# Attention and two feed-forward blocks on one core: weight work assigned to other steps, and the second token block's operands made at other times and on another engine

## The chip, the cores and the metric

One Trainium2 chip, one of its cores. The time of a kernel is the device time of one launch in microseconds (us); several runs are made and their median is given. The engines named below are TensorE (PE, the matrix engine), VectorE (DVE), ScalarE (ACT), GpSimd (POOL) and SyncE (SP), whose queue issues nearly all DMAs.

## The reference

Three parts follow each other on 2304 tokens (4 sequences of 576) of 512 features:

```python
# attention, 8 heads of 64
cum    = np.cumsum(np.maximum(s, 0), axis=-1)
scores = q @ k.T / sqrt(64) + np.minimum(-(cum[..., None] - cum[..., None, :]), 0)
x      = softmax(causal(scores)) @ v          # 2304 x 512
# first block, 512 -> 2048 -> 512
h = x @ w_in;  x = np.maximum(0.01 * h, h) @ w_out
# second block, 512 -> 2048 -> 512, with weights of its own
h = x @ w_in2; y = (np.maximum(h, 0) + np.log1p(np.exp(-np.abs(h)))) @ w_out2
```

The weights come as 64-bit floats, which the kernel turns into 32-bit floats with integer operations.

## The kernel before, in words

Every product is made from a high and a low part of each operand (hi x hi, hi x lo, lo x hi, three products on PE). High parts are made by a copy on ACT, low parts by a subtraction on DVE or POOL.

**Attention** takes the first quarter of the span (to about 244 us) and is not touched.

**The first block** (the "first half" of what follows) runs over 68 steps, written out in `steps`. The 16 blocks of 128 hidden units are taken in four groups of four (`G = 4`): group 0 has 8 steps for the tokens that attention left over (2 chunks of 384, steps 0 to 7), groups 1 to 3 have 20 steps each (5 chunks of 512, 512, 256, 512 and 512 tokens, four hidden blocks each), beginning at steps 8, 28 and 48 (`begin`). A step n (loop at L898) does, in this order: the products into a hidden bank (`h_mm`, L145); the work that was put off to this step (`tick`); the leaky activation on ACT (L826); the entries of `plan` for this step; and the output products of step n - 3 (`out_mm`, L846). After the fourth hidden block of a chunk, `out_mm` adds four banks to `acc` on DVE (L853; a copy on ACT in group 0). Output products rotate through five banks of which a chunk needs four, so the next chunk's first output step needs the banks that these additions free.

All engines take their instructions in the order in which this program issues them. What stands in `plan` (L856 to L896) is:
- `own` (L864): the conversions (`split_w`) of this block's weights for the next group, eight per group, "i" for the input weights and "o" for the output weights. DVE does three or four instructions (L114 to L123), ACT three, POOL one or two.
- `spare` (L872 to L877): the 32 conversions (`prepare`) of the second block's weights, in the order of `blocks`: (j, e, "i" or "o") for j = 0 to 7. `prepare` is put on step n: two ACT instructions (L728, L729) then, the four DVE instructions of `convert` (L732 to L735) in step n + 1, the high part on ACT (L708) in n + 1 and the low part on POOL (L712) in n + 2, with two stores to `w2d` in DRAM by SP. The second "i" block of a pair also brings four half-width sums on DVE at step n + 2 (L751 to L757), which make two more operands. The raw load of a block is issued two steps ahead, into one of four buffers.
- the operands of the second block's first token block (L883 to L896), from step 59 on: sums on DVE (L794), high parts on ACT (L797), low parts on DVE or POOL (L801).

Before, `spare` spread 22 of the 32 blocks evenly over the free steps of groups 1 and 2, and 10 over the first 13 steps of group 3.

**The second block** (the "second half") does its input products as seven instead of eight products of half-size blocks: four token chunks in two token blocks (`sb` 0 and 1, `PAIRS`), operands B11, B12, B21, B22 and the sums T1 = B12 - B11, T2 = B22 - T1, T3 = B22 - B12, T4 = B21 - T2. Seven operands (B12 is only used in sums) are split into high and low parts, which lie in eight places of `xh` and `xl` (`slots`, `home`); the sums overwrite their sources in `acc`. `Quad(sb, j)` does the seven products (L1013) for two hidden blocks and joins them on DVE (L1030); four `Unit`s then make the activation: four ACT instructions, then DVE (L958, L961), POOL `correct` (L964), ACT high part (L970), POOL low part (L974). `outputs` multiplies by the output weights (L1068) and DVE adds to `acc` (L1076). A `Plain` does the same for the 256 tokens that are in neither block, with ordinary products (L1095). `emit_out` and the plain products share three banks.

The order is a list of events with a time `t` (`on`), sorted at the end; one unit of `t` is meant as one product of a quad. Quad n's products take 7 units; then come the outputs of quad n - 1 (8 units), the plain products (2.1) and the outputs of the plain before (2). The second token block's operands are made around quad 7 (`t7`, L1140 to L1148): four sums and four low parts, for each of two halves (`kp`), on DVE; the other three low parts on POOL. `fetch` loads the prepared weights back from `w2d`, on SP: "i" 6 units ahead of a quad, "o" 1 unit after its start.

Of the kernel before, what the change touches and what calls it, by code (L numbers as in the profile page):

```python
# [13 lines left out]
F32R = mybir.dt.float32r  # L14
AF = mybir.ActivationFunctionType
ALU = mybir.AluOpType
PSUM = bass.MemoryType.PSUM

P = 128
# [12 lines left out]
def attn_moe_moe(ctx, tc, q, k, v, s, w1i, w1o, w2i, w2o, out):  # L32
    nc = tc.nc
# [7 lines left out]
    NG = NF // G  # L41
# [9 lines left out]
    def pool(name, bufs=1, **kw):  # L51
        return tc.tile_pool(name=name, bufs=bufs, **kw)
# [616 lines left out]
    enter = lambda stage, nm, **kw: stages[stage].enter_context(pool(nm, **kw))  # L669
# [26 lines left out]
    begin = {}  # L696
# [4 lines left out]
    NJ = NF // 2  # L701
# [61 lines left out]
    def split_x(c):  # L763
# [7 lines left out]
    slots = [(r, c) for c in (*PAIRS[0], *PAIRS[1]) for r in (0, 2)]  # L771
    home = [
        {"B11": 0, "T2": 1, "T3": 2, "T1": 3, "B21": 4, "T4": 5, "B22": 6},
        {"B11": 7, "T2": 0, "T3": 1, "T1": 2, "B21": 3, "T4": 4, "B22": 5},
    ]
    PRODUCTS = [
        ("A11", "B11"), ("S2", "T2"), ("S3", "T3"), ("S1", "T1"), ("A12", "B21"), ("A22", "T4"), ("S4", "B22")
    ]

    def operand(sb, nm, kp):  # L780
        r, c = slots[home[sb][nm]]
        c = slice(c, c + 512)
        return xh[:, r + kp, c], xl[:, r + kp, c]

    def source(sb, nm, kp):
        i, k = {"B11": (0, 0), "T1": (0, 0), "T2": (0, 0), "B12": (1, 0), "T3": (1, 0), "B21": (0, 2), "T4": (0, 2), "B22": (1, 2)}[nm]
        c = PAIRS[sb][i]
        return acc[:, k + kp, c:c + 512]

    def combine(sb, nm, kp, queue=nc.vector):  # L790

        a, b = {"T1": ("B12", "B11"), "T3": ("B22", "B12"), "T2": ("B22", "T1"), "T4": ("B21", "T2")}[nm]
        a, b = source(sb, a, kp), source(sb, b, kp)
        queue.tensor_tensor(source(sb, nm, kp), a, b, op=ALU.subtract)  # L794

    def x_high(sb, nm, kp):
        nc.scalar.activation(operand(sb, nm, kp)[0], source(sb, nm, kp), AF.Copy)  # L797

    def x_low(sb, nm, kp, queue=nc.vector):
        hi, lo = operand(sb, nm, kp)  # L800
        queue.tensor_tensor(lo, source(sb, nm, kp), hi.bitcast(F32), op=ALU.subtract)  # L801
# [56 lines left out]
    def at(n, fn, *args):  # L858
        plan.setdefault(n, []).append((fn, args))

    taken = set()
    for g in range(1, NG):
        a = begin[g - 1]
        own = (2, 5, 8, 11, 15, 18, 16, 19) if g > 1 else (None,) * 4 + (3, 6, 4, 7)  # L864
        for j, n in enumerate(own):
            if n is not None:
                w = (0, g * G + j // 2, "io"[j % 2])
                at(max(a + n - 2, 0), load_w, *w)
                at(a + n, split_w, *w, (1, 1, 1, 1, 2, 2))
                taken.add(a + n)  # L870
    blocks = [(j, e, nm) for j in range(NJ) for e, nm in ((0, "i"), (1, "i"), (0, "o"), (1, "o"))]
    a, z = begin[1], begin[NG - 1]  # L872
    spare = [[n for n in r if n not in taken] for r in (range(a, z), range(z, z + 13))]
    spare = [r[k * len(r) // m] for r, m in zip(spare, (22, 10)) for k in range(m)]
    for n, x in zip(spare, blocks):
        at(max(n - 2, 0), load_w, 1, 2 * x[0] + x[1], x[2])
        at(n, prepare, n, *x)  # L877
# [5 lines left out]
    k = begin[NG - 1, chunks[1]] + G + LAG  # L883
    z = len(steps) - 1
    follow = {"B11": "T1", "T1": "T3", "T3": "T2"}
    for nm, n in (("B11", k), ("T1", k + 2), ("T3", k + 4), ("B21", k + 5), ("T2", k + 6), ("T4", z - 1), ("B22", z)):
        for kp in range(2):
            m = min(n + kp, z)
            if nm == "T4":
                at(m, combine, 0, nm, kp)  # L890
            at(m, x_high, 0, nm, kp)
            at(m, x_low, 0, nm, kp, nc.gpsimd if nm in ("T3", "B21") else nc.vector)
            if nm in follow:
                at(m, combine, 0, follow[nm], kp)
# [19 lines left out]

    wpools.append(enter(1, "wpool1", bufs=2))
    lpool = enter(1, "lpool", bufs=3, side="right")
    gpools = [enter(1, "gpool1", bufs=3, side="right"), gpool]
    order = [0]
    events = []
# [2 lines left out]
    def on(t, fn, *args):  # L922
        events.append((t, len(events), fn, args))
# [63 lines left out]
    class Quad:  # L987
# [13 lines left out]
        def product(self, n, name):  # L1001
            a, b = PRODUCTS[n]
            if name not in self.ps:
                tag, bufs = next(banks["ps_h"]) if self.first_one else TAGS[name]
                self.ps[name] = psA.tile([P, 512], F32, tag=tag, name="ps_h", bufs=bufs)
            k, half = {"A11": (0, 0), "A12": (0, 1), "A21": (1, 0), "A22": (1, 1),
                       "S1": (2, 0), "S2": (2, 1), "S3": (3, 0), "S4": (3, 1)}[a]
            wh, wl = ready[self.sb, self.j, "i"][k]
            for kp in range(2):
                w = slice(half * HALF + kp * P, half * HALF + (kp + 1) * P)  # L1010
                hi, lo = operand(self.sb, b, kp)
                for m, (x, y) in enumerate(((wh[:, w], hi), (wh[:, w], lo), (wl[:, w], hi))):
                    nc.tensor.matmul(  # L1013
                        self.ps[name], x, y, start=n < 4 and kp == 0 and m == 0, stop=kp == 1 and m == 2,
                        skip_group_check=n >= 4,
                    )
# [96 lines left out]
    quads = [Quad(sb, j) for sb in range(2) for j in range(NJ)]  # L1113
    plains = [Plain(j) for j in range(NJ)]
    t = 0
    for n, q in enumerate(quads):
        q.at(t)
        if n + 1 < len(quads):
            j = quads[n + 1].sb, quads[n + 1].j
            on(t - 6 if n else -1, fetch, *j, "i")  # L1120
            on(t + 1, fetch, *j, "o")
        if n == NJ - 1:
            t7 = t
        t += 7
        if n == 0:
            for i in range(LAG, 0, -1):
                on(t, out_mm, len(steps) - i)
                t += 2
        else:
            quads[n - 1].outputs(t)  # L1130
            t += 8
        if n < NJ:
            plains[n].at(t)
            t += 2.1
        if 0 < n <= NJ:
            plains[n - 1].outputs(t)
            t += 2
    quads[-1].outputs(t)

    for kp in range(2):  # L1140
        b = t7 + 1.25 * kp
        for n, nm in ((-8, "B11"), (3.2, "T1"), (5.7, "T3"), (8.2, "T2"), (10.7, "B21"), (13.2, "T4"), (15.7, "B22")):
            if nm in ("T2", "T4"):
                on(b + n - 0.9, combine, 1, nm, kp)
            on(b + n, x_high, 1, nm, kp)
            on(b + n + 0.8, x_low, 1, nm, kp, nc.gpsimd if nm in ("T3", "B21", "B22") else nc.vector)
        on(b - 5, combine, 1, "T1", kp)
        on(b - 2, combine, 1, "T3", kp)  # L1148

    for t, _, fn, args in sorted(events, key=lambda x: x[:2]):  # L1150
        fn(*args)
# [48 lines left out]
```

## Time and profile before

| | us |
|---|---|
| median of 3 runs (lowest, highest) | 962.31 (961.06, 964.36) |
| the profiled execution | 961.56 |
| its span, first to last instruction | 959.8 |
| PE busy, of the span | 945.1 |
| DVE busy | 672.5 |
| ACT busy | 574.7 |
| POOL busy | 553.2 |

The profile is of one execution. Busy times of PE include the overlap of pipelined products, so a pause is seen best from the start of one product to the start of the next. "x12" in a row is a count; what stands behind "<-" in brackets is the idle time in front of an instruction and what ended it. L numbers are lines of the kernel.

### The profile page before, as it was taken

To read this page: it belongs to the slowest core of one execution; us is meant where nothing else is said; L and a number is where in the kernel's file an instruction comes from. 1 tells how busy PE (TensorE), PEld (TensorE's weight loads), DVE (VectorE), ACT (ScalarE), POOL (GpSimd) and SP (SyncE) were. 2 spreads that over 40 slices of the span, in tenths; PEclk is the share of its full clock that TensorE was granted. 3 is DMA by queue.
4 is the path that set the end of the run, shared out by engine and by line. 5 is a ranking of instruction groups with operands and counts; after the bars stand their busy time and mean duration, and the time that the engine had idled before them with its cause. 6 is when DMAs were issued, how large, how long until landed. Compare 5 with 4: busy or idle time off the path is not lost.

```text
span 959.8 us, 15357 instructions
## 1 busy us (share of the span) xinstructions
PE 945.1 (98%) x5173; PEld 767.8 (80%) x5173; DVE 672.5 (70%) x1306; ACT 574.7 (60%) x1185; POOL 553.2 (58%) x536
## 2 busy tenths in 40 slices
PE   9999999999999999998999999999999999999998
PEld 6666767777998888887888888888888778888887
DVE  8888556554267998899667945666666976666666
ACT  6888677665465655555445546666556565565563
POOL 7778556444357677657745734644444674455543
PEclk9999999999999999999999999999999999999999
DMA  7453433321736754566555445342425238445402
GB/s 242 150 163 126 148 113 125 134 89 37 277 110 206 228 188 149 177 202 209 165 196 176 155 140 167 99 145 65 155 66 175 88 131 314 146 132 168 140 0 88
DMA packets 79251, 143.61 MB, mean 150 GB/s; under 512 B 7626, under 2 KB 24906, under 8 KB 79172
## 3 DMA queue, kind: packets, MB, share of 16 engines
q1 hardware_dynamic: 78740, 141.87, 45.0%
q8 instruction: 41, 0.67, 0.3%
q10 hardware_dynamic: 432, 0.75, 0.2%
q14 instruction: 38, 0.31, 0.1%
HBM read 109.33 MB, written 33.25 MB: 149 GB/s over the span
## 4 chain that ended last, share of the span: by engine, by line
PE 77%; DVE 12%; POOL 4%; issue 3%; ACT 2%; DMA 1%; SPq 0%; DVEq 0%; POOLq 0%; ACTq 0%
PE ps_out L1068 18%; PE ps_h L145 15%; PE ps_h L1013 14%; PE ps_out L846 12%; PE pt_s L316 4%; PE pt_t L377 3%; PE ps_o L635 3%; PE pt_v L409 3%; PE ps_h L1095 2%; DVE ws L734 2%; PE pt_s L409 1%; DVE ws L733 1%; DVE ws L732 1%; DVE acc L853 1%; POOL l L964 1%
## 5 line engine op out<-in xcount | busy, mean ns | idle before, releaser
L964 POOL TENSOR_TENSOR l<-l,e 128x512 f32<-128x512 f32 x72 | 94.4, 1311 | 173.4 <-DVE e L961 160.0
L151 POOL TENSOR_TENSOR gl<-gf,gh 128x512 fp32r<-128x512 f32 (+2 forms) x68 | 88.6, 1304 | 123.2 <-ACT gh L150 82.6
L360 POOL TENSOR_SCALAR sc<-sc,st 128x512 f32<-128x512 f32 (+4 forms) x160 | 89.3, 570 | 79.8 <-DVE st L356 62.0
L145 PE MATMUL ps_h<-xh,wih 128*128 128x512 f32 (+2 forms) x320 | 119.9, 375 | 0.0
L1076 DVE TENSOR_TENSOR acc<-ps_out,acc 128x512 f32<-128x512 f32 (+1 forms) x127 | 86.7, 684 | 46.2 <-PE ps_out L1068 44.0
L145 PE MATMUL ps_h<-xh,wil 128*128 128x512 f32 (+2 forms) x320 | 118.1, 369 | 0.0
L145 PE MATMUL ps_h<-xl,wih 128*128 128x512 f32 (+2 forms) x320 | 117.9, 369 | 0.0
L1068 PE MATMUL ps_out<-woh,gh 128*128 128x512 f32 x290 | 112.7, 389 | 1.7 <-DVE acc L1076 1.7
L1068 PE MATMUL ps_out<-wol,gh 128*128 128x512 f32 x290 | 112.4, 388 | 0.0
L349 ACT ACTIVATE sc<-sc,st 128x512 f32<-128x512 f32 (+2 forms) x144 | 83.4, 582 | 35.0 <-DVE st L337 29.2
L846 PE MATMUL ps_out<-gh,woh 128*128 128x512 f32 (+2 forms) x272 | 100.1, 368 | 4.3 <-DVE acc L853 4.1
L846 PE MATMUL ps_out<-gh,wol 128*128 128x512 f32 (+2 forms) x272 | 99.6, 366 | 0.0
L846 PE MATMUL ps_out<-gl,woh 128*128 128x512 f32 (+2 forms) x272 | 99.5, 366 | 0.0
L826 ACT ACTIVATE gf<-ps_h 128x512 f32<-128x512 f32 (+2 forms) x68 | 37.0, 544 | 102.9 <-PE ps_h L145 93.9
L974 POOL TENSOR_TENSOR gl<-l,gh 128x512 fp32r<-128x512 f32 x72 | 95.0, 1329 | 5.2 <-ACT gh L970 5.2
L1068 PE MATMUL ps_out<-woh,gl 128*128 128x512 f32 x290 | 88.8, 388 | 0.0
L1013 PE MATMUL ps_h<-xh,wih 128*128 128x512 f32 x224 | 87.5, 391 | 0.9 <-DVE ps_h L1030 0.8
L1013 PE MATMUL ps_h<-xl,wih 128*128 128x512 f32 x224 | 87.2, 389 | 0.0
L1013 PE MATMUL ps_h<-xh,wil 128*128 128x512 f32 x224 | 87.2, 389 | 0.0
L970 ACT ACTIVATE gh<-l 128x512 fp32r<-128x512 f32 x72 | 45.3, 630 | 66.1 <-POOL l L964 66.1
L337 DVE CUSTOM_DVE_ANT_0 sc<-pt_s,mask 128x512 f32<-128x512 f32 (+3 forms) x129 | 59.1, 482 | 16.4 <-PE pt_t L377 15.4
L145 PEld LDWEIGHTS ps_h<-xh,wil 128*128 128x128 f32 x320 | 60.2, 188 | 9.6
(161 smaller groups left out, 2345.2 us busy)
## 6 DMA issues: line engine op xcount, KB each, us to landing
w2d<-stg SPq DMA_DIRECT2D x88, 256.0 KB
rawi<-in_moe_w_in SPq DMA_DIRECT2D x32, 512.0 KB
rawo<-in_moe_w_out SPq DMA_DIRECT2D x32, 512.0 KB
wih<-w2d SPq DMA_DIRECT2D x64, 256.0 KB
wil<-w2d SPq DMA_DIRECT2D x64, 256.0 KB
woh<-w2d SPq DMA_DIRECT2D x32, 256.0 KB
wol<-w2d SPq DMA_DIRECT2D x32, 256.0 KB
K<-in_k SPq DMA_DIRECT2D x15, 432.0 KB
```

The costliest lines, as they stand in the source:

```text
L145: nc.tensor.matmul(ps, a, b, start=kk == 0 and n == 0, stop=kk == KD - 1 and n == 2)
L151: nc.gpsimd.tensor_tensor(gl, gf, gh.bitcast(F32), op=ALU.subtract)
L337: nc.vector.tensor_tensor_reduce(out=self.sc[:, j, c], in0=self.ps[j][:, c], in1=m, scale=-scale, scalar=low, op0=ALU.add, op1=ALU.min, ac ...
L349: nc.scalar.activation(x, x, AF.Exp, scale=-1.0, bias=self.stat(0, e + self.last), accum_out=self.stat(1, e))
L360: nc.gpsimd.tensor_scalar(x, x, self.stat(2, e), 1.0, op0=ALU.mult, op1=ALU.mult)
L846: nc.tensor.matmul(ps, a, b, start=f == 0 and m == 0, stop=f == G - 1 and m == 2)
L964: nc.gpsimd.tensor_tensor(self.l, self.l, self.e, op=ALU.subtract)
L970: nc.scalar.activation(self.gh, self.l, AF.Copy)
L974: nc.gpsimd.tensor_tensor(self.gl, self.l, self.gh.bitcast(F32), op=ALU.subtract)
L1013: nc.tensor.matmul(self.ps[name], x, y, start=n < 4 and kp == 0 and m == 0, stop=kp == 1 and m == 2, skip_group_check=n >= 4,)
L1068: nc.tensor.matmul(u, a, v, start=m == 0, stop=m == len(ops) - 1)
L1076: nc.vector.tensor_tensor(d[..., w], o[..., w], d[..., w], op=ALU.add)
```

## The change

It has two parts.

**First half.** `own` of groups 2 and 3 moves: "i" 8 and 12 from step 2 of the group before to step 1, "o" from 5 to 4, "i" 9 and 13 from 8 to 7. `spare` is written out: one block at step 1 and one at step 5 (in group 0), ten in each of groups 1 to 3.

| group begins at | blocks before (offset in the group) | blocks after |
|---|---|---|
| 0 | none | 1, 5 |
| 8 | 0, 1, 3, 4, 6, 7, 9, 10, 12, 13, 14 | 0, 2, 3, 5, 6, 9, 12, 13, 14, 17 |
| 28 | 0, 1, 3, 4, 6, 7, 9, 10, 12, 13, 14 | 0, 2, 3, 5, 6, 9, 12, 13, 14, 17 |
| 48 | 0, 1, 2, 3, 5, 6, 7, 9, 10, 11 | 0 to 7, 9, 12 |

Offsets 8 to 11 are the steps of 256 tokens.

**Second half.** For the second token block: B21 gets a place of its own (`xpool`, 8 KB of each partition), so that B11 and B21 can be split during quads 1 and 4. The sums are made in the order T3 = B22 - B12, T2 = T3 + B11, T1 = B22 - T2, T4 = B21 - T2; T1 now overwrites T3. T3, T2 and T4 are summed on POOL during quads 2, 3 and 5, T1 on DVE in quad 7. The high and low parts of T2, T3, T1, T4 and B22 are made in quad 7's round; all low parts but T1's on POOL. The outputs of plains 2 to 5 move by most of a round, to stand between the products of a quad and the outputs of the quad before; those of plains 0, 1, 6 and 7 stay where they were.

```diff
     home = [
         {"B11": 0, "T2": 1, "T3": 2, "T1": 3, "B21": 4, "T4": 5, "B22": 6},
-        {"B11": 7, "T2": 0, "T3": 1, "T1": 2, "B21": 3, "T4": 4, "B22": 5},
+        {"B11": 7, "T2": 0, "T3": 1, "T1": 2, "B21": 8, "T4": 3, "B22": 4},
     ]
...
-        a, b = {"T1": ("B12", "B11"), "T3": ("B22", "B12"), "T2": ("B22", "T1"), "T4": ("B21", "T2")}[nm]
+        a, b = {"T1": ("B22", "T2") if sb else ("B12", "B11"), "T3": ("B22", "B12"),
+                "T2": ("T3", "B11") if sb else ("B22", "T1"), "T4": ("B21", "T2")}[nm]
+        op = ALU.add if sb and nm == "T2" else ALU.subtract
         a, b = source(sb, a, kp), source(sb, b, kp)
-        queue.tensor_tensor(source(sb, nm, kp), a, b, op=ALU.subtract)
+        queue.tensor_tensor(source(sb, nm, kp), a, b, op=op)
...
-        own = (2, 5, 8, 11, 15, 18, 16, 19) if g > 1 else (None,) * 4 + (3, 6, 4, 7)
+        own = (1, 4, 7, 11, 15, 18, 16, 19) if g > 1 else (None,) * 4 + (3, 6, 4, 7)
...
-    a, z = begin[1], begin[NG - 1]
-    spare = [[n for n in r if n not in taken] for r in (range(a, z), range(z, z + 13))]
-    spare = [r[k * len(r) // m] for r, m in zip(spare, (22, 10)) for k in range(m)]
+    spare = [1, 5]
+    for g in range(1, NG):
+        some = (0, 2, 3, 5, 6, 9, 12, 13, 14, 17) if g < NG - 1 else (0, 1, 2, 3, 4, 5, 6, 7, 9, 12)
+        spare += [begin[g] + n for n in some]
...
+    extra.append(enter(1, "xpool").tile([P, 2, 2, 512], F32R, tag="xp", name="xp"))
...
-        if n == NJ - 1:
-            t7 = t
+        starts.append(t)
         t += 7
+        if 3 < n < NJ:
+            plains[n - 2].outputs(t)
+            t += 2
...
-        if 0 < n <= NJ:
+        if n in (1, 2, NJ - 1, NJ):
             plains[n - 1].outputs(t)
             t += 2
...
     for kp in range(2):
-        b = t7 + 1.25 * kp
-        for n, nm in ((-8, "B11"), (3.2, "T1"), (5.7, "T3"), (8.2, "T2"), (10.7, "B21"), (13.2, "T4"), (15.7, "B22")):
-            if nm in ("T2", "T4"):
-                on(b + n - 0.9, combine, 1, nm, kp)
+        b = starts[NJ - 1] + 1.7 * kp
+        for n, nm in ((2.2, "T2"), (5.6, "T3"), (9.8, "T1"), (13.4, "T4"), (16.8, "B22")):
             on(b + n, x_high, 1, nm, kp)
-            on(b + n + 0.8, x_low, 1, nm, kp, nc.gpsimd if nm in ("T3", "B21", "B22") else nc.vector)
-        on(b - 5, combine, 1, "T1", kp)
-        on(b - 2, combine, 1, "T3", kp)
+            on(b + n + 0.8, x_low, 1, nm, kp, nc.vector if nm == "T1" else nc.gpsimd)
+        on(b + 8.4, combine, 1, "T1", kp)
+        for n, nm in enumerate(("B11", "T3", "T2", "B21", "T4"), 1):
+            b = starts[n] + 2.4 * kp
+            if nm[0] == "T":
+                on(b + 5, combine, 1, nm, kp, nc.gpsimd)
+            else:
+                on(b + 3, x_high, 1, nm, kp)
+                on(b + 5, x_low, 1, nm, kp, nc.gpsimd)
```

## Rows read from the trace of the kernel before

**Rows 1.** The page, busy us of each engine, share of the span, instructions.

```profile
PE 945.1 (98%) x5173; PEld 767.8 (80%) x5173; DVE 672.5 (70%) x1306; ACT 574.7 (60%) x1185; POOL 553.2 (58%) x536
```

**Rows 2.** Stretches: length, then PE, PEld, DVE, ACT, POOL busy, granted clock, DMA.

```profile
244.00:272.00 28.00, 28.00 (x162) 27.82 (x161) 8.73 (x14) 15.91 (x32) 12.78 (x11) 1.00 0.74 253
343.69:346.85 3.16, 3.02 (x14) 2.17 (x12) 3.13 (x7) 2.53 (x5) 1.30 (x1) 1.00 0.45 168
433.50:445.60 12.10, 10.17 (x56) 8.53 (x55) 11.38 (x8) 6.30 (x12) 12.10 (x9) 1.00 0.66 210
442.83:450.08 7.25, 4.38 (x13) 3.23 (x12) 7.04 (x9) 2.77 (x5) 5.44 (x4) 0.76 0.64 217
546.08:550.38 4.30, 3.03 (x14) 2.17 (x13) 4.30 (x7) 2.87 (x7) 4.28 (x4) 1.00 0.87 293
550.38:749.00 198.62, 198.62 (x956) 167.84 (x955) 123.84 (x189) 112.69 (x195) 95.98 (x74) 1.00 0.39 127
749.00:802.46 53.46, 50.85 (x230) 40.71 (x229) 42.57 (x62) 35.82 (x64) 35.30 (x27) 1.00 0.40 131
```

**Rows 3.** Waits of PE: waiter, releaser, us in total, times, longest.

```profile
PE ps_out L846 <- DVE acc L853: 4.1, 2, 2.9
PE ps_out L1068 <- DVE acc L1076: 1.7, 2, 1.4
```

**Rows 4.** The chain that ended last, in order of time: start, us, what.

```profile
256.75 2.08 PE ps_out L846 x12
...
512.82 2.72 PE ps_out L846 x12
...
696.96 9.52 PE ps_h L1013 x42
...
717.36 2.87 PE ps_h L1095 x24
...
722.98 8.18 PE ps_h L1013 x36
...
802.46 9.52 PE ps_h L1013 x42
```

**Rows 5.** DVE in order of time: start, us, line, operation, idle before.

```profile
433.81 1.26 DVE L732 TENSOR_SCALAR ws<-ws 128x512 f32<-128x512 f32 x1 [0.88 <-ACT ws L728]
...
444.62 1.53 DVE L735 CUSTOM_DVE_ANT_0 ws<-ws,wt 128x1024 uint16<-128x1024 uint16 x1
...
534.84 0.42 DVE L732 TENSOR_SCALAR ws<-ws 128x512 f32<-128x512 f32 x1
...
537.52 1.78 DVE L801 TENSOR_TENSOR xl<-acc,xh 128x512 fp32r<-128x512 f32 x1
...
774.57 1.76 DVE L794 TENSOR_TENSOR acc<-acc 128x512 f32<-128x512 f32 x1 [1.85 <-POOL xl L801]
```

**Rows 6.** Groups of DVE instructions, 244 to 575 us: count, busy us, mean ns.

```profile
L735 DVE CUSTOM_DVE_ANT_0 ws<-ws,wt 128x1024 uint16<-128x1024 uint16 x32 | 40.0, 1251 | 4.3
...
L733 DVE TENSOR_SCALAR ws<-ws 128x512 int32<-128x512 int32 x32 | 25.4, 793 | 1.1
L732 DVE TENSOR_SCALAR ws<-ws 128x512 f32<-128x512 f32 x32 | 21.9, 686 | 16.2 <-ACT ws L728 13.0 <-POOL stg L712 3.2
...
L734 DVE SCALAR_TENSOR_TENSOR ws<-rawo,ws 128x512 int32<-128x512 int32 x16 | 17.3, 1084 | 0.6
```

**Rows 7.** ACT in order of time, the first read of a raw load.

```profile
253.07 0.66 ACT L108 ACTIVATE wm<-rawi 128x512 f32<-128x512 f32 x1
```

**Rows 8.** SP's queue in order of time, the first raw loads of this half.

```profile
245.51 0.98 SPq L93 DMA_DIRECT2D rawi<-in_moe_w_in  x2
```

**Rows 9.** Groups of DVE instructions, 572 to 960 us.

```profile
L801 DVE TENSOR_TENSOR xl<-acc,xh 128x512 fp32r<-128x512 f32 x11 | 9.9, 914 | 1.9 <-ACT xh L797 1.9
L794 DVE TENSOR_TENSOR acc<-acc 128x512 f32<-128x512 f32 x8 | 8.6, 1076 | 1.9 <-POOL xl L801 1.9
```

**Rows 10.** Groups of POOL instructions, 572 to 960 us.

```profile
L801 POOL TENSOR_TENSOR xl<-acc,xh 128x512 fp32r<-128x512 f32 x6 | 7.9, 1328 | 1.4 <-ACT xh L797 1.4
```

More of the change, by code (lines that the diff above doesn't have):

```diff
@@ L780, in operand @@
     def operand(sb, nm, kp):
-        r, c = slots[home[sb][nm]]
+        n = home[sb][nm]
+        if n == 8:
+            return extra[0][:, kp, 0], extra[0][:, kp, 1]
+        r, c = slots[n]
         c = slice(c, c + 512)
         return xh[:, r + kp, c], xl[:, r + kp, c]
+    extra = []
+    WHERE = {"B11": (0, 0), "B12": (1, 0), "B21": (0, 2), "B22": (1, 2), "T4": (0, 2)}
     def source(sb, nm, kp):
-        i, k = {"B11": (0, 0), "T1": (0, 0), "T2": (0, 0), "B12": (1, 0), "T3": (1, 0), "B21": (0, 2), "T4": (0, 2), "B22": (1, 2)}[nm]
+        i, k = {**WHERE, "T1": (sb, 0), "T2": (0, 0), "T3": (1, 0)}[nm]
         c = PAIRS[sb][i]
@@ L1115, in attn_moe_moe @@
     t = 0
+    starts = []
     for n, q in enumerate(quads):
```

## The prediction, made before the change was run

> **What bounds the kernel now.** I read the page first: the matrix engine (PE) is busy for 945.1 us, 98% of the span [rows 1], so only time in which PE waits can be won. The waits of PE then name the vector engine (DVE): accumulations into acc that come late, at L853 in the first half and at L1076 in the second [rows 3]. The table of stretches says where: none from 550.38 to 749, but in three output steps of the first half and from 749 to 802.46 [rows 2].
>
> Idle time understates the loss, because the products behind a pause start slowly; I measure from start to start, each stretch cut from the first product of an output step to the first of the next. An undisturbed output step of twelve 512-wide products takes 2.72 us [rows 4]. The step that began at 343.69 took 3.16 (lost 0.44); the one at 442.83 took 7.25 (lost 4.53; its granted clock is 0.76 on the mean, so part of it ran at 1.2 instead of 2.4 GHz behind the pause); the one at 546.08 took 4.30 (lost 1.58) [rows 2]. In the second half a round (quad, outputs of the quad before, plain products, plain outputs) takes 722.98 - 696.96 = 26.02 us. The round of quad 8 has no plain products (2.87), so from 722.98 two rounds and a shorter one end at 722.98 + 26.02 + 26.02 + 23.15 = 798.17; quad 9 begins at 802.46, so 4.29 are lost around quads 6 to 8 [rows 4]. **Together 0.44 + 4.53 + 1.58 + 4.29 = 10.84 us.**
>
> **Why DVE is late.** In steps 41 and 42 two converts of four instructions each run back to back from 433.81 to 446.15, and the accumulations that free the banks follow them [rows 5]. That is 6.2 us for a convert where the mean rows give 0.69 + 0.79 + 1.08 + 1.25 = 3.81 [rows 6]. GpSimd (POOL) worked for all 12.10 us of that stretch [rows 2]. The same instruction (L732) took 1.26 us at 433.81 and 0.42 at 534.84, that of L801 1.78 at 537.52 [rows 5] and 0.91 on the mean of the second half [rows 9]. So DVE's work between SBUF operands has two prices, by what POOL does beside it.
>
> **The change, first half.** The number of instructions, products and bytes stays; only their step moves.
> - *Two blocks go to steps 1 and 5 of the first group.* There DVE is busy for 8.73 of 28 us and ACT for 15.91 [rows 2]; two converts are 7.6 us of DVE. The first of their loads would be issued at 245.51, where two loads of that size and line were issued before [rows 8]; the first of those was read at 253.07 [rows 7], so one needs at most 7.6 us. ACT would ask for it at about 249. If it landed as late as 253.07, ACT's next parts would be 4 us late; they are used by the output step at 256.75 [rows 4]. I take nothing, with 0 and 2 us lost as bounds. The stores of the halves now stand on SP's queue ahead of later loads; those are asked for two steps on, so that is free as well.
> - *Steps 8 to 19 and 28 to 39* lose two blocks each (8 become 6), and of their four 256-wide steps two now have no block. That is 7.6 us less for DVE in each, and fewer low parts for POOL. So step 40 is reached without a queue: before, ACT came late to it and DVE waited 0.88 us for ACT ahead of the two converts [rows 5]. The blocks of steps 40, 41 and 42 themselves keep their places. The group before has the same pattern at steps 19 to 22 and lost 0.44 there. I take that value for both groups, as the nearest row: **-4.09 us** (bounds -4.97, the two pauses gone, and 0).
> - *Third group:* block (7, "i") goes from steps 55 and 57 to 54 and 55, its sums from 59 to 57, the "o" blocks from 58 and 59 to 57 and 60. From step 59 to the bank that step 63 needs, DVE did two converts, the sums and eight operand instructions of L794 and L801, six of them at about 1.7 (the first is shown [rows 5]). One convert (3.81) and the sums leave, against 1.58 lost: **-1.58 us** (bounds -1.58 and 0, since the last convert now stands among the L801 work).
> Moving the weight splits by one to four steps changes no buffer's last reader; it costs nothing as long as the lead of two steps, some 8 us, covers a load (7.6 at most). If not, ACT stands by the difference.
>
> **Second half.** Around quads 6 to 8 DVE made eight sums (L794, 1.08 us on the mean) and eight low parts (of L801's eleven, at 0.91): 15.9 us by these rows [rows 9], in 53.46 us of which it was busy for 42.57 [rows 2]. Now two sums and two low parts, those of T1, stay (4.0 us). Six sums and the low parts of B11 and B21 go to POOL under quads 1 to 5, ten instructions at 1.33 [rows 10], 13.3 us where POOL is busy for 95.98 of 198.62 [rows 2]. What they delay is the low part of a unit, which the plan wants 7.7 units of 1.36 us (half an output step), some 10 us, ahead of its use: hidden, unless several pile up. At the boundary POOL has eight low parts instead of six, +2.7 us on 35.30 of 53.46 [rows 2]. ACT's fourteen high parts keep their cost; four of them go to quads 1 and 4.
> Late next may be the sum of T1: it overwrites T3 and so waits for T3's low part on POOL, with the accumulations queued behind it on DVE and PE waiting for their banks. Such a wait is in the trace, 1.85 us at 774.57 [rows 5], and a PE pause of 1.4 on L1076 [rows 3]. The new plan leaves 2 units (2.7 us) between the two. I leave 0.5 us of the 4.29 for it: **-3.79 us** (bounds -4.29, and a loss of 1.4 for one more such pause).
> Plain outputs of quads 2 to 5 stand ahead of the quad outputs: the same products. The reload of the "o" weights waits on SP for these outputs, 8 units or 11 us; the next "i" load stands 12 units behind it in the plan, and both are used a round later. Nothing, as long as that round covers it. The boundary round becomes 2.75 us longer and the third shorter.
>
> **Sum.** 4.09 + 1.58 + 3.79 = 9.46 us. The profiled execution took 961.56 us; 961.56 - 9.46 = 952.1. The median of the runs, 962.31, is 0.75 above it, so **952.8**.
>
> A rule speaks against the first term. The Trainium skill, page "SBUF — State Buffer", section "Who interferes with whom", says that a DVE instruction with two SBUF inputs or in a two-port mode shares one port pair with GpSimd, and that the loser blocks for the whole instruction. By it the two converts cost what POOL does beside them, backlog or not: the term is 0 and the sum 956.9. The trace agrees on the price (1.26 against 0.42 on L732), but the same two converts one group earlier cost PE 0.44 and not 4.53.
>
> **Rivals.**
> A. *The converts at steps 41 and 42 stay slow beside POOL.* For it: their blocks do not move. Against: the group before. Then 952.8 + 4.1 = 956.9.
> B. *The boundary waits for POOL* (T1's sum, or the low parts of T4 and B22). For it: the 1.85 us wait, and POOL gets more. Against: DVE loses 11.9 us and feeds POOL sooner. Then 952.8 + 3.8 = 956.6.
> C. *Both, so that the change doesn't do what its lists of steps suggest:* about 961.
> D. *Slower: the first raw load.* The place is step 1: ACT waits in order for a load issued at 245.51 ahead of 1 MB accumulator loads; behind ACT stand the parts that the output step at 256.75 needs. It decides from a landing after about 253, one us for each us. Slower by 0.3% needs 9.5 + 2.9 = 12.4 us more, a landing after 265. Against: the 7.6 us. Then about 966.
>
> **How the numbers follow.** A measurement of this kernel can tell about 0.3%, 2.9 us, from no change. Forecast 0.70, A 0.10, B 0.10, C 0.06, D 0.04: faster 0.90 (forecast, A, B), same 0.06 (C), slower 0.04 (D). The range goes down to 961.56 - 10.84 = 950.7 (nothing left of the pauses), rounded to 950.0, and up to A and B with a further us, 958.0; C and D stay outside.
>
> **What would show it.** No PE wait on L853 above 1 us; the step after 442.83 at some 3.2 us with a granted clock of 1.0; quads 7 to 9 in an unbroken row of rounds; L794 six times on POOL and twice on DVE; DVE near 31 us in the boundary stretch. Wrong would be a new PE wait in the 30 us after 244, or one near quad 8 that follows a POOL instruction of L801.

## The result and the profile after

The changed kernel takes **952.16 us** (median of 6 runs, 951.81 to 952.27), the kernel before 961.10 in runs beside it (6 runs): ratio 0.9901, 95% interval 0.9886 to 0.9917. It is 8.94 us faster. The profiled execution took 951.81, its span is 950.0.

The page, busy time of each engine, against [rows 1]; then the waits of PE that name the accumulations, against [rows 3] (L1086 is the old L1076, L861 the old L853):

```profile
PE 941.3 (99%) x5173; PEld 767.3 (81%) x5173; DVE 668.0 (70%) x1294; ACT 575.8 (61%) x1185; POOL 564.3 (59%) x548
```

```profile
PE ps_out L1078 <- DVE acc L1086: 0.8, 1, 0.8
...
PE ps_out L854 <- DVE acc L861: 0.3, 1, 0.3
```

PE executes the same 5173 products. Twelve instructions went from DVE to POOL, and 5.8 us of waiting on accumulations became 1.1.

The stretches that answer to [rows 2], cut in the same way (length, then PE, PEld, DVE, ACT, POOL busy, granted clock, DMA): the three output steps, the second half up to quad 7, and quads 7 and 8 up to quad 9.

```profile
342.85:345.57 2.72, 2.72 (x14) 2.25 (x12) 2.69 (x3) 1.72 (x3) 2.26 (x2) 1.00 0.67 193
441.55:444.27 2.72, 2.72 (x14) 2.25 (x12) 2.65 (x4) 1.71 (x3) 2.72 (x2) 1.00 0.61 182
540.25:543.58 3.33, 3.01 (x14) 2.17 (x12) 3.33 (x7) 2.86 (x7) 1.60 (x3) 1.00 0.93 298
543.58:739.30 195.72, 195.72 (x944) 165.42 (x943) 119.03 (x182) 114.16 (x198) 110.04 (x86) 1.00 0.38 125
739.30:792.51 53.21, 52.44 (x242) 43.27 (x241) 36.97 (x55) 34.86 (x61) 33.42 (x27) 1.00 0.43 146
```

The first two output steps are now undisturbed at 2.72 us, from 3.16 and 7.25. The third takes 3.33, 0.61 too long, from 4.30. The rounds stand in the chain (start, us, what), against [rows 4]:

```profile
739.46 9.55 PE ps_h L1023 x42
...
763.93 2.88 PE ps_h L1105 x24
766.82 2.74 PE ps_out L1078 x12
769.55 9.52 PE ps_h L1023 x42
779.08 13.60 PE ps_out L1078 x60
792.67 9.52 PE ps_h L1023 x42
```

Quad 9 follows quad 8 and the outputs behind it without a gap: 769.55 + 9.52 + 13.60 = 792.67. Quad 7's round, one plain output longer than a usual one, should last 9.52 + 13.60 + 2.87 + 2.75 = 28.74 and lasts 769.55 - 739.46 = 30.09, so 1.35 is lost there, from 4.29. **Of 10.84 us of pauses 0.61 + 1.35 = 1.96 are left**; the 8.88 that went fit the 8.94 of the medians, for which the ratio's interval gives 8.0 to 11.0.

Why those two are left is in DVE's order of time, near 540 and near 757:

```profile
537.47 1.84 DVE L809 TENSOR_TENSOR xl<-acc,xh 128x512 fp32r<-128x512 f32 x1 [1.37 <-ACT xh L805]
539.24 1.78 DVE L802 TENSOR_TENSOR acc<-acc 128x512 f32<-128x512 f32 x1
540.94 1.40 DVE L861 TENSOR_TENSOR acc<-ps_out,acc 128x256 f32<-128x256 f32 x4
...
755.52 1.41 DVE L802 TENSOR_TENSOR acc<-acc 128x512 f32<-128x512 f32 x1
756.85 1.78 DVE L809 TENSOR_TENSOR xl<-acc,xh 128x512 fp32r<-128x512 f32 x1
758.56 0.68 DVE L1086 TENSOR_TENSOR acc<-ps_out,acc 128x512 f32<-128x512 f32 x1
```

Both times two instructions between SBUF operands stand ahead of the accumulations at their slow price. In the second case DVE waits for nothing: the sum of T1 and its low part run 3.2 us beside a POOL instruction of 1.75 at 756.33.

### The profile page after: what moved, and what is told of

It reads as the page before. It is cut to its first block, busy times and chain, and to the rows that moved or that the text cites. A ratio compares the mean times of both kernels' runs of the same rounds, so it can differ in the third digit from the quotient of the medians.

```text
span 950.0 us, 15346 instructions
## 1 busy us (share of the span) xinstructions
PE 941.3 (99%) x5173; PEld 767.3 (81%) x5173; DVE 668.0 (70%) x1294; ACT 575.8 (61%) x1185; POOL 564.3 (59%) x548
## 4 chain that ended last, share of the span: by engine, by line
PE 93%; DVE 3%; POOL 1%; ACT 1%; issue 1%; DMA 0%; SPq 0%; DVEq 0%; POOLq 0%; ACTq 0%
PE ps_h L145 20%; PE ps_out L1078 20%; PE ps_out L854 17%; PE ps_h L1023 16%; PE pt_s L316 4%; PE pt_t L377 3%; PE ps_o L635 3%; PE pt_v L409 3%; PE ps_h L1105 2%; PE pt_s L409 1%; PE pt_t L372 1%; PE pt_s L302 1%; DVE sc L337 1%; POOL sc L360 0%; ACT sc L349 0%
## 5 line engine op out<-in xcount | busy, mean ns | idle before, releaser
L1086 DVE TENSOR_TENSOR acc<-ps_out,acc 128x512 f32<-128x512 f32 (+1 forms) x127 | 86.8, 685 | 42.5 <-PE ps_out L1078 40.0
L1023 PE MATMUL ps_h<-xh,wih 128*128 128x512 f32 x208 | 81.0, 389 | 0.0
L1023 PE MATMUL ps_h<-xl,wih 128*128 128x512 f32 x208 | 81.0, 389 | 0.0
L1023 PE MATMUL ps_h<-xh,wil 128*128 128x512 f32 x208 | 80.9, 389 | 0.0
```

The lines of the kernel that those rows point to most:

```text
L1023: nc.tensor.matmul(self.ps[name], x, y, start=n < 4 and kp == 0 and m == 0, stop=kp == 1 and m == 2, skip_group_check=n >= 4,)
L1086: nc.vector.tensor_tensor(d[..., w], o[..., w], d[..., w], op=ALU.add)
```

## The experiments

**Each half of the change alone.** The first takes the kernel before and puts in the new `own` and `spare`; the second takes the changed kernel and puts the old ones back (the second's edit, in part):

```diff
-        own = (1, 4, 7, 11, 15, 18, 16, 19) if g > 1 else (None,) * 4 + (3, 6, 4, 7)
+        own = (2, 5, 8, 11, 15, 18, 16, 19) if g > 1 else (None,) * 4 + (3, 6, 4, 7)
...
+    spare = [r[k * len(r) // m] for r, m in zip(spare, (22, 10)) for k in range(m)]
```

> The kernel before with the first half's new lists of steps (own, spare) alone. My theory (both parts work separately, each removes its own pauses): the output steps of the first half lose less than 1 us together instead of 6.55, the pauses around quads 6 to 8 stay at about 4.3; time 961.1 - 6 = about 955. Rival A (the converts of steps 41 and 42 stay slow, and the time came from the second half): about 959.

> The changed kernel with the old lists of steps in the first half. My theory: the first half keeps its pauses of about 6.5 us, the boundary loses about 1.4 us as in the changed kernel instead of 4.3; time 961.1 - 3 = about 958. Rival B (the boundary waits for POOL as much as it waited for DVE): about 961.

First half alone: 955.41 us (954.96 to 955.80), ratio 0.9944 (0.9929 to 0.9959). Second half alone: 958.31 (958.07 to 958.52), ratio 0.9973 (0.9963 to 0.9983), both against 960.89. They save 5.48 and 2.58, together 8.06, near the 8.94 of both. The waits of PE, first half alone and then second half alone, show one half's pauses each:

```profile
PE ps_out L1069 <- DVE acc L1077: 1.7, 2, 1.4
PE ps_h L1014 <- DVE ps_h L1031: 1.2, 1, 1.2
```

```profile
PE ps_out L854 <- DVE acc L861: 4.1, 2, 2.9
...
PE ps_out L1077 <- DVE acc L1085: 0.8, 1, 0.8
```

**The plain outputs back at their old places** (the block `if 3 < n < NJ` taken out, `if 0 < n <= NJ` put back), and **the early sums on DVE**:

```diff
-                on(b + 5, combine, 1, nm, kp, nc.gpsimd)
+                on(b + 5, combine, 1, nm, kp)
```

> The changed kernel with the plain outputs of quads 2 to 5 at their old places. My theory: their move only makes the boundary round 2.75 us longer, so that its work has more room; without it the work of T1 on DVE meets the same pace of accumulations, and the pause near quad 7 grows by less than 1 us: 952 to 953. A rival that makes their move a main part of the gain: 954 or more.

> The changed kernel with the six early sums (T3, T2, T4 under quads 2, 3 and 5) on DVE instead of POOL, at the same places. My theory: what counts is that they are spread over rounds in which DVE has 40% to spare, not the engine: 952 to 952.5. Rival (the engine counts, since each sum holds the accumulations behind it by up to 1.2 us): pauses at quads 2, 3 and 5, 954 or more.

951.92 (951.57 to 952.41) and 952.33 (952.12 to 954.38). The pause near quad 7 is in both profiles (1.06 and 1.36 us too long, 1.35 in the changed kernel's), and nothing new. Without the longer round it did not grow but was 0.3 us shorter. Neither the move of the plain outputs nor the engine of the early sums is worth anything that can be measured.

**The engine alone**: the first half's lists, and the second half as before but with its eight sums on POOL.

```diff
-                on(b + n - 0.9, combine, 1, nm, kp)
+                on(b + n - 0.9, combine, 1, nm, kp, nc.gpsimd)
...
-        on(b - 5, combine, 1, "T1", kp)
+        on(b - 5, combine, 1, "T1", kp, nc.gpsimd)
```

> The kernel of the first experiment (new lists of steps in the first half) with all eight sums of the second token block on POOL instead of DVE, at their old times around quad 7, and nothing else of the second half changed. My theory: the gain comes from doing the work earlier, in rounds with room; at the boundary POOL would have 10.6 us more, and DVE's low parts behind these sums wait for it: 954 to 957 against 955.4. Rival (the engine is what counts): 952.5, as the changed kernel.

957.22 (956.12 to 957.73), where the same kernel with the sums on DVE took 955.41. PE waits longer for the join, and DVE is not busy but idle in front of it:

```profile
PE ps_h L1014 <- DVE ps_h L1031: 2.0, 1, 2.0
```

```profile
752.20 1.27 DVE L801 TENSOR_TENSOR xl<-acc,xh 128x512 fp32r<-128x512 f32 x1 [3.46 <-ACT xh L797]
753.40 0.68 DVE L1031 TENSOR_TENSOR ps_h<-ps_h,u 128x512 f32<-128x512 f32 x1
754.00 0.68 DVE L801 TENSOR_TENSOR xl<-acc,xh 128x512 fp32r<-128x512 f32 x1
```

The sums stand on POOL's queue ahead of a unit's `correct`. ACT's copy for that unit begins 0.9 us later behind the quad's first product (750.94 behind 743.77, against 748.99 behind 742.73 with the sums on DVE); the operand's high part comes behind it, and DVE stands 3.46 us at the low part with the join behind it.

This is only part of the 1.8 us between the medians. From quad 7's first product to quad 9's the profiles have 54.68 and 53.78 us, so 0.9 more. Another 1.0 us went at 270, in the first half, which the same first half did not lose in the first experiment; the account below says why. So the engine alone wins nothing. What the second half wins comes from the rest of its change: the earlier times, the new order of the sums, and the low parts of B11, T2 and T4 that left DVE. No run takes these apart.

**Backlog or price.** Is DVE late at the two converts of steps 41 and 42 because of the work ahead of them (backlog), or because they run slowly beside POOL (price)? Four kernels take the output step of step 43 apart (lost 4.53 before, 0 after). The edits are cut; `now` holds the step's number.

```diff
@@ the kernel before: low parts of steps 39 to 43 copied on ACT @@
-            nc.gpsimd.tensor_tensor(lo, src, hi.bitcast(F32), op=ALU.subtract)
+            if 39 <= now[0] <= 43:
+                nc.scalar.activation(lo, src, AF.Copy)
+            else:
+                nc.gpsimd.tensor_tensor(lo, src, hi.bitcast(F32), op=ALU.subtract)
@@ the changed kernel: group 2 with offset 10 instead of 17 @@
-        some = (0, 2, 3, 5, 6, 9, 12, 13, 14, 17) if g < NG - 1 else (0, 1, 2, 3, 4, 5, 6, 7, 9, 12)
+        some = (0, 2, 3, 5, 6, 9, 12, 13, 14, 17) if g < 2 else (0, 2, 3, 5, 6, 9, 10, 12, 13, 14) if g == 2 else (0, 1, 2, 3, 4, 5, 6, 7, 9, 12)
@@ the changed kernel: more DVE work at step 39 @@
+            for _ in range(10 if j == 4 else 1):
+                nc.vector.tensor_tensor(S1, A21, A22, op=ALU.add)
@@ the changed kernel: more POOL work at step 39 @@
+            for _ in range(4 if now[0] == 39 else 1):
+                nc.gpsimd.tensor_tensor(lo, src, hi.bitcast(F32), op=ALU.subtract)
```

> The kernel before, with the low parts of the second block's weights that fall in steps 39 to 43 (group 2) made as plain copies on ACT instead of differences on POOL; they are therefore not the reference's low parts, and the amount of work is the same but for the engine. DVE's own work and its order stay. Theory 'slow beside POOL' (rival A's mechanism): the converts of steps 41 and 42 get faster than 6.2 us and the pause of that step falls from 4.5 us to below 1: time 961 - 4 = about 957. Theory 'backlog' (DVE arrives late at step 41 because of the blocks before): the pause stays near 4.5 us, 961.

> The changed kernel with one block of group 2 moved from offset 17 back to offset 10, a 256-wide step, so that three of the four short steps have weight work; offsets 12, 13 and 14 keep a block each. Theory 'backlog': DVE and ACT reach step 41 late again and the output step of step 43 loses 2 to 4.5 us: 954 to 956.5. Theory 'slow beside POOL' alone: the converts of steps 41 and 42 are as before, so no more than 0.5 us: 952.5.

> The changed kernel with 3.8 us more work for DVE alone at step 39: the first half-width sum of pair 4 is made ten times instead of once, with the same result. That is as much DVE time as one more convert there, but no work for POOL or ACT. Theory 'backlog' (DVE comes late to steps 41 and 42): the output step of step 43 loses 2 us or more, 954 to 956. Theory 'slow beside POOL': DVE had 2.8 us to spare ahead of these converts, and their price stays, so less than 1.5 us: 952 to 953.5.

> The changed kernel with 3.9 us more work for POOL alone at step 39: one low part is made four times instead of once, with the same result. No work is added for DVE or ACT. Theory 'slow beside POOL': POOL's queue reaches without a gap over the converts of steps 41 and 42, both cost about 6 us, and the output step of step 43 loses 2 us or more: 954 to 956. Theory 'backlog': DVE comes no later, less than 1 us: 952 to 953.

They took 956.18 (ratio 0.9956, 0.9941 to 0.9971), 954.98 (0.9942, 0.9927 to 0.9957), 953.78 (0.9923, 0.9908 to 0.9937) and 953.60 (0.9919, 0.9902 to 0.9935). In the profiles the pause ahead of this step's second bank is gone in the first, and 2.05, 1.50 and 1.47 us in the others. (In the fourth's profile attention took 2 us more, so all its times stand later.) In each profile, the first convert's start and the accumulations that follow the second one stand in DVE's order of time. The kernel before (its start is in [rows 5]), the changed kernel, then the four in this order:

```profile
446.08 1.40 DVE L853 TENSOR_TENSOR acc<-ps_out,acc 128x256 f32<-128x256 f32 x4
```

```profile
430.47 0.61 DVE L732 TENSOR_SCALAR ws<-ws 128x512 f32<-128x512 f32 x1 [2.80 <-ACT ws L728]
...
440.17 1.40 DVE L861 TENSOR_TENSOR acc<-ps_out,acc 128x256 f32<-128x256 f32 x4
```

```profile
433.43 0.43 DVE L736 TENSOR_SCALAR ws<-ws 128x512 f32<-128x512 f32 x1 [2.00 <-ACT ws L732]
...
441.23 1.41 DVE L857 TENSOR_TENSOR acc<-ps_out,acc 128x256 f32<-128x256 f32 x4
```

```profile
431.72 1.26 DVE L732 TENSOR_SCALAR ws<-ws 128x512 f32<-128x512 f32 x1 [0.89 <-ACT ws L728]
...
444.00 1.41 DVE L861 TENSOR_TENSOR acc<-ps_out,acc 128x256 f32<-128x256 f32 x4
```

```profile
432.16 0.43 DVE L732 TENSOR_SCALAR ws<-ws 128x512 f32<-128x512 f32 x1
...
443.64 1.41 DVE L862 TENSOR_TENSOR acc<-ps_out,acc 128x256 f32<-128x256 f32 x4
```

```profile
430.75 0.94 DVE L758 TENSOR_TENSOR ws<-ws 128x256 f32<-128x256 f32 x1 [2.56 <-POOL stg L713]
...
433.77 1.44 DVE L734 TENSOR_SCALAR ws<-ws 128x512 f32<-128x512 f32 x1 [0.22 <-ACT ws L730]
...
445.38 0.75 DVE L863 TENSOR_TENSOR acc<-ps_out,acc 128x256 f32<-128x256 f32 x2
```

"Lead" is the time from the first convert's start to the point at which PE, without a pause, would begin with the second bank; "pair" is the time from that start to the accumulations.

| kernel | lead | pair | pair - lead | pause |
|---|---|---|---|---|
| before | 9.70 | 12.27 | 2.57 | 3.03 |
| changed | 11.76 | 9.70 | -2.06 | 0 |
| before, low parts on ACT | 9.18 | 7.80 | -1.38 | 0 |
| changed, block at offset 10 | 10.70 | 12.28 | 1.58 | 2.05 |
| changed, DVE + 3.8 us | 10.44 | 11.48 | 1.04 | 1.50 |
| changed, POOL + 3.9 us | 10.61 | 11.61 | 1.00 | 1.47 |

The pause is pair minus lead plus 0.46, in all four kernels that have one. The first kernel came out as 'slow beside POOL' had it, the second as 'backlog' had it, and the last two lie between the two forecasts. So neither theory was the whole: the change won 2.06 us of lead and 2.57 us of price. Taking POOL's low parts away is enough by itself, with DVE's own blocks as they were. More work for DVE alone, or for POOL alone, brings back 1.5 us each, and each moves both columns: late DVE work holds POOL's queue (its L123 starts at 432.28 instead of 428.25), which then lies over the converts; long POOL work makes DVE wait (2.56 us at L758) and start late. The two expectations that gave each theory a result of its own were too simple.

**The two pauses that are left.**

```diff
-            on(b + n + 0.8, x_low, 1, nm, kp, nc.vector if nm == "T1" else nc.gpsimd)
+            on(b + n + 0.8, x_low, 1, nm, kp, nc.gpsimd)
...
-        some = (0, 2, 3, 5, 6, 9, 12, 13, 14, 17) if g < NG - 1 else (0, 1, 2, 3, 4, 5, 6, 7, 9, 12)
+        some = (0, 2, 3, 5, 6, 9, 12, 13, 14, 17) if g < NG - 1 else (0, 1, 2, 3, 4, 5, 6, 7, 9, 15)
```

> The changed kernel with T1's two low parts on POOL instead of DVE. The profile after shows the pause near quad 7 (1.4 us) behind T1's second sum and first low part on DVE, 1.41 and 1.78 us beside a POOL instruction. My theory: without the low part DVE reaches the accumulation 1.7 us sooner and the pause goes: 951. Rival (POOL, now with ten low parts in that round, delivers the units late): 952 or more.

> The changed kernel with the last weight block at offset 15 of group 3 (step 63) instead of 12 (step 60). The profile after shows the last pause of the first half (0.6 us) behind the second low part and the sum of L809 and L802 at 1.8 us each, which the convert of step 61 put 2.2 us later. My theory: the pause goes, 951.5. Rival (those instructions wait for ACT's high parts and for POOL, not for the convert): no change, 952.2; or a new pause later, where operands of the next block are due: more.

> The changed kernel with both of the changes that took a pause away: T1's low parts on POOL and the last weight block at step 63. If the two pauses (1.4 and 0.6 us) are separate, 952.2 - 1.2 - 0.4 = about 950.5, faster than both kernels.

T1's low parts on POOL: 951.00 (950.76 to 951.53), the pause near quad 7 is gone. The last block at step 63: 951.77 (951.23 to 952.55), the pause at 541 is gone, and the low part before it takes its fast price:

```profile
537.51 0.69 DVE L809 TENSOR_TENSOR xl<-acc,xh 128x512 fp32r<-128x512 f32 x1 [2.89 <-ACT xh L805]
538.12 0.68 DVE L802 TENSOR_TENSOR acc<-acc 128x512 f32<-128x512 f32 x1
```

It starts no earlier (537.51 against 537.47, with the output step at 540.28 and 540.25) and still behind ACT's high part, so the 2.2 us of lateness in the expectation were not the cause. What is gone beside it is the block's low part on POOL (L712), which began at 537.47 in the profile after. By the medians alone the second of these kernels is not told from no change. Both together: **950.16** (949.86 to 951.38), ratio 0.9886 (0.9871 to 0.9901) to the kernel before, 2.0 us below the changed kernel. From the first block on PE never stands idle in that profile: no two products start more than 0.24 us apart.

## Why the prediction was right, and where a term was off

952.8 was forecast, 952.16 measured, within the range; 9.46 us off the pauses were forecast, 8.88 went. That the total is so near is in part luck: the terms were off by 0.88 one way and by 0.61 and 0.85 the other, and the base, 962.31, was a median of three runs where six gave 961.10. Term by term:

- *Steps 8 to 39 to other places, -4.09:* the two steps lost 0.44 and 4.53 before and lose nothing after, so -4.97, the far bound. I had left 0.44 in each, as the nearest row. What failed is that I took that row for a property of steps 19 to 22; by the rows it hung on what stood ahead and on POOL's queue, both of which the change thins. The first convert and the accumulations of that group, before and after:

```profile
333.61 0.43 DVE L732 TENSOR_SCALAR ws<-ws 128x512 f32<-128x512 f32 x1 [0.51 <-ACT ws L728]
...
344.20 1.41 DVE L853 TENSOR_TENSOR acc<-ps_out,acc 128x256 f32<-128x256 f32 x4
```

```profile
331.77 0.43 DVE L732 TENSOR_SCALAR ws<-ws 128x512 f32<-128x512 f32 x1 [2.81 <-ACT ws L728]
...
339.33 1.40 DVE L861 TENSOR_TENSOR acc<-ps_out,acc 128x256 f32<-128x256 f32 x4
```

  The pair fell from 10.59 to 7.56 us and the lead rose from 10.76 to 11.76. No run changes one of the two alone in this group.
- *Third group, -1.58:* measured 1.58 - 0.61 = -0.97. The bound named the cause (the last convert among the L801 work), and moving that block took the rest away, by way of the low part on POOL that belongs to it.
- *Second half, -3.79:* 4.29 - 1.35 = -2.94. I had left 0.5 for the sum of T1 waiting for POOL. That wait did not come: the two T1 instructions cost 1.41 and 1.78 us beside POOL instead, and taking the low parts off DVE removed the pause. The place was right, the mechanism and the size were not. DVE's busy time in the stretch fell from 42.57 to 36.97, not to 31: I took twelve instructions off it at their mean price (sixteen, less the four of T1), but five of the sixteen began ahead of 749, from 740.55 to 748.83. So seven left (62 became 55), and T1's four cost 4.7 us, not 4.0.
- *Two blocks at steps 1 and 5, 0:* nothing was lost in the profile after, but by a narrow margin. The first raw load, issued at 244.67, was late for ACT by 1.14 us. Later ACT copies banks into `acc`, and PE's next bank follows:

```profile
249.26 0.66 ACT L728 ACTIVATE ws<-rawi 128x512 f32<-128x512 f32 x1 [1.14 <-DMA rawi<-in_moe_w_in]
...
268.02 1.62 ACT L859 ACTIVATE acc<-ps_out 128x384 f32<-128x384 f32 x4
```

```profile
268.75 0.33 PE L854 MATMUL ps_out<-gh,woh 128*128 128x384 f32 x1
```

  The kernel with the engine alone changed has the same first half. In its profile the load was issued at 245.31, and ACT could read it 5.74 us later instead of 4.59:

```profile
251.05 0.66 ACT L728 ACTIVATE ws<-rawi 128x512 f32<-128x512 f32 x1 [2.29 <-DMA rawi<-in_moe_w_in]
...
269.79 1.61 ACT L851 ACTIVATE acc<-ps_out 128x384 f32<-128x384 f32 x4
```

```profile
270.31 0.44 PE L846 MATMUL ps_out<-gh,woh 128*128 128x384 f32 x1 [0.76 <-ACT acc L851]
```

  PE lost 1.0 us there, within the bounds of 0 and 2. The product began 0.52 us behind ACT's first copy; in the profile after it began 0.73 behind it, so about 0.2 us were to spare. So in that profile rival D's mechanism was at work: a landing near 251 cost something, not only one after 253, and the place was not the output step at 256.75 but the bank at 270.
- *The plain outputs, 0:* shown by their experiment; so is the "o" reload that waits behind them.
- *Six sums and four low parts to POOL under quads 1 to 5, hidden:* PE has no pause from 543.58 to 739.30 with POOL busy for 110.04 of 195.72 us.

Rival A was right about its price and wrong about its conclusion. The rule of the Trainium skill ("SBUF — State Buffer", "Who interferes with whom") that GpSimd and a two-input or two-port DVE instruction exclude each other fits the experiment that took POOL's low parts away: the pair of converts fell from 12.27 to 7.80 us. But the price was not fixed by the steps, since fewer blocks ahead of them also shortened POOL's queue. Rival B's pause was there at a third of its size, but DVE waited for nothing in front of it; a wait for POOL's queue showed only when all sums went to POOL at the old times.

## What to carry to other kernels

Where two engines share work between SBUF operands, count for each wait how early the late engine starts and what its instructions cost beside the other one; a list that thinned a crowded stretch gained on both here. Moving the sums to another engine at the same times won nothing (957.2 against 955.4). With the sums made earlier, where both engines have room, the engine made no difference (952.2 and 952.3). A place that shows no pause can still be near one: look at how much was to spare, as for the first load. After a change, look at what stands directly ahead of the instructions that free a bank: two more edits of that kind gave 2 us here.

## What was not expected

The granted clock fell behind some pauses and not behind others. PE had stood idle for 2.87 us in the kernel before, for 1.89 with the block at offset 10, and for 2.05 with all sums on POOL at the old times; the stretches behind these had a mean granted clock of 0.58, 0.52 and 0.59, at which products start 0.43 us apart instead of 0.23, and that added up to 1.7 us to the loss. Behind the pauses of 1.27 and 1.42 us it stayed at 1.00. Three rows of the kernel before, behind 446.54, 548.19 and 776.99, then one each of the other two kernels:

```profile
446.54:450.08 3.54, 3.54 (x9) 2.85 (x10) 3.47 (x6) 2.42 (x5) 2.66 (x2) 0.58 0.46 172
548.19:550.38 2.19, 2.19 (x10) 1.80 (x11) 2.19 (x4) 1.96 (x6) 2.17 (x3) 1.00 0.97 338
776.99:779.20 2.21, 2.21 (x10) 1.83 (x11) 2.21 (x4) 1.05 (x3) 0.33 (x1) 1.00 0.94 341
```

```profile
444.47:448.00 3.53, 3.53 (x9) 2.76 (x10) 3.46 (x6) 2.43 (x5) 2.66 (x2) 0.52 0.43 162
```

```profile
754.14:758.30 4.16, 4.16 (x11) 3.29 (x12) 2.33 (x4) 4.01 (x9) 3.95 (x4) 0.59 0.00 0
```

These are single profiles. That a pause of such a length always brings the fall is not shown.
